# Moving the subtractions of a split-precision kernel from GpSimd to VectorE, and its gate the other way

## The chip, the core and the metric

The kernel runs on one core of one Trainium2 chip. Five engines work side by side, each with its own queue that it takes in order: TensorE (PE: matrix products and transposes), VectorE (DVE), ScalarE (ACT), GpSimd (POOL) and SyncE (SP), which issues nearly all DMAs. The metric is the time in microseconds that the device takes for one execution. Three executions took 1071.99, 1073.51 and 1075.36 us; their median is 1073.51 us.

## The reference

Three stages follow each other. Attention has 4 batches, 8 heads, 576 positions and 64 columns a head; a forget gate's running sum is a bias on the scores. Its output, 2304 tokens of 512 columns, runs through two layers with 2048 hidden columns each. The second layer's weights are as large as the first's.

```python
s_pos = np.maximum(s, 0.0)
cum = np.cumsum(s_pos, axis=-1)
bias = -(cum[:, :, :, None] - cum[:, :, None, :])
scores = np.where(causal, -1000000000.0, scores + np.minimum(bias, 0.0))
...
def _moe_ref(x, w_in, w_out, s, b):
    h = x @ w_in
    r = np.maximum(h, 0.0)
    g = s * (r * r) + b            # the gate: a scale and a bias, one number each
    return (g @ w_out).astype(np.float32)

def _moe2_ref(x, w_in, w_out, alpha):
    h = x @ w_in
    g = np.maximum(h, 0.0) + alpha * np.minimum(h, 0.0)
    return (g @ w_out).astype(np.float32)
```

The weights of the layers arrive as 64-bit floats, and the kernel reads them as pairs of 32-bit words.

## The kernel before

**Hi and lo parts.** TensorE multiplies in a reduced form of 32-bit floats. To keep the precision, a tensor x is split: ScalarE copies it into that form (hi), and another engine subtracts hi from x (lo). That is the helper `split` (L105 to L107): L106 is ScalarE's copy, L107 the subtraction, on VectorE unless the caller names GpSimd. A product of two split tensors is three products, hi by hi, hi by lo and lo by hi.

**Packets.** A packet is 128 of the hidden columns of a layer: a piece of w_in and a piece of w_out, 512 KB each, sixteen packets a layer. `load_packet` (L157) issues the two loads on SyncE (L174, L178), turns the 64-bit floats of each piece into 32-bit floats in `convert` (L116 on ScalarE, then L117 and L118 on VectorE), and splits them; here the lo parts are made on GpSimd (L191, and so L107 on POOL, tile w). Each piece is converted and split before the next.

**Blocks.** Tokens are taken 256 at a time (narrow) or 512 (wide). Layer 1 has seven narrow blocks and a last wide one, layer 2 one narrow block and four wide ones. `inputs` and `wide_inputs` (L547, L573) split a block's tokens. For each packet `up` (L623) multiplies the tokens by w_in into a PSUM tile hp (L634), and ScalarE takes it out with Relu (L653). In layer 1 ScalarE then squares it (L655) and VectorE applies the gate, times s plus b (L656), with s and b as columns of one number a partition; in layer 2 ScalarE takes the negative part out as well (L660) and VectorE joins the two (L661). The result r is split at L664 into gh and gl (tiles gh and gl in narrow blocks of layer 1, ring elsewhere; in the wide block of layer 1 the profile calls both ring). `down` (L667) multiplies gh and gl by w_out into accumulators (L673 in layer 1, L683 in layer 2), and it comes two packets after its `up` in layer 1, three in layer 2. Before the change the lo part gl is made on GpSimd in all of layer 1 and in layer 2's narrow block, and on VectorE in layer 2's wide blocks.

**Attention** works in units, a pair of heads by one of two ranges of rows. On VectorE it prepares the bias (L365), transposes q and k (L311), and joins scores and bias with a running minimum (L391); ScalarE takes the exponent (L397); on VectorE two small steps make the reciprocal of the sums (L402, L403), and GpSimd normalises (L406, tile probs), after which TensorE transposes (L437, tile pt) and multiplies by v (L453). GpSimd also masks (L369), clears (L361) and makes lo parts of v (tile vs_all).

**What sets the order.** The program is written as one stream in which attention and layer 1 alternate by a pace; the framework then reorders the instructions of each engine by a schedule of its own, which is made ahead of time and weighs each operation by the engine that it is on. So an operation that moves to another engine can shift everything around it, on all engines. Layer 1's first block and its sixteen packets stand beside attention's first batch; layer 2's packets are loaded and converted from the wide block of layer 1 on, into slots that layer 1's packets leave.

Of the kernel before, what the change touches and what calls it, by code (L numbers as in the profile page):

```python
# [8 lines left out]
F32 = mybir.dt.float32  # L9
# [9 lines left out]
def tile_forget_attention__then__two_mlps(  # L19
# [20 lines left out]
    nc = tc.nc  # L40
# [64 lines left out]
    def split(hi, lo, src, lo_eng=nc.vector):  # L105
        nc.scalar.copy(hi, src)  # L106
        lo_eng.tensor_tensor(out=lo, in0=src, in1=hi.bitcast(F32), op=ALU.subtract)  # L107
# [39 lines left out]
    def weight_tiles(f):  # L147

        if f not in SPARE:
            return [slot(n, F32R, f"w1_{f}_{n}") for n in SPLIT[SLOT[f]]]  # L150
        tiles = []
        for tag, pool, cols, n in SPARE[f]:
            t = pool.tile([P, cols], F32R, tag=tag, name=f"w1_{f}_{len(tiles)}")
            tiles += [t[:, i * 512 : (i + 1) * 512] for i in range(n)]
        return tiles

    def load_packet(layer, f):  # L157
        w_in, w_out = ((w_in1, w_out1), (w_in2, w_out2))[layer]


        def raw(name, n):
            if layer == 1:
                if f % 2:
                    tile_ = one.tile([P, 1024], U32, tag=("xh0", "xl0")[n], name=name)
                else:
                    tile_ = two.tile([P, 1088], U32, tag="probs", name=name)
            else:
                pool, tag = RAW[2 * f + n]
                tile_ = pool.tile([P, 1024], U32, tag=tag, name=name)
            return tile_[:, :1024].rearrange("p (n z) -> p n z", z=2)  # L170

        wi = raw(f"wi{layer}_{f}", 0)
        wo = raw(f"wo{layer}_{f}", 1)
        nc.sync.dma_start(  # L174
            out=wi.rearrange("p (c n) z -> p c (n z)", c=NCC),
            in_=w_in[:, f * 2 * P : (f + 1) * 2 * P].rearrange("(c p) n -> p c n", p=P),
        )
        nc.sync.dma_start(out=wo.rearrange("p n z -> p (n z)"), in_=w_out[f * P : (f + 1) * P, :])  # L178
        t = weight_tiles(f) if layer == 1 else []
        for n, src in enumerate((wi, wo)):  # L180
            if layer == 1:
                pool, tag, cols = WT[(2 * f + n) % len(WT)]
                wt = pool.tile([P, cols], U32, tag=tag, name=f"wt{f}_{n}")[:, :512]
            elif (f, n) == (NF - 1, 1):
                wt = two.tile([P, 512], U32, tag="ph", name="last")
            else:
                wt = slot(WHOLE[f][n], U32, f"wt0_{f}_{n}")
            convert(src, wt)
            if layer == 0:
                t += [slot(m, F32R, f"w0_{f}_{len(t)}_{m}") for m in SPLIT[f][2 * n : 2 * n + 2]]  # L190
            split(t[2 * n], t[2 * n + 1], wt.bitcast(F32), nc.gpsimd)  # L191
        return [x.rearrange("p (c n) -> p c n", c=NCC) for x in t[:2]] + t[2:]


# [352 lines left out]
    def inputs(layer, t):  # L547

        first, count = SIZES[layer][t]
        if count == 2:  # L550
            return wide_inputs(layer, t, first)
        if layer == 0:
            src = xf.pop(t)
            xh = one.tile([P, NCC, T], F32R, tag=f"xh{t % 2}", name=f"xh{layer}_{t}")
            xl = one.tile([P, NCC, T], F32R, tag=f"xl{t % 2}", name=f"xl{layer}_{t}")
            xh, xl = ([x[:, c] for c in range(NCC)] for x in (xh, xl))
        else:
            src = one.tile([P, NCC, T], F32, tag="res", name=f"x2_{t}")
            nc.sync.dma_start(out=src, in_=x2_d[t].rearrange("p (c n) -> p c n", n=T))

            xh, xl = (
                [
                    two.tile([P, T], F32R, tag=tag, name=f"x{tag}{layer}_{t}_{c}", bufs=3 if c < 3 else 2)
                    for c, tag in enumerate(tags)
                ]
                for tags in (("gh", "gh", "gh", "r"), ("gl", "gl", "gl", "r"))
            )
        for c in range(NCC):
            on_pool = layer == 0 and (t or c % 2)
            split(xh[c], xl[c], src[:, c], nc.gpsimd if on_pool else nc.vector)  # L570
        return xh, xl

# [37 lines left out]
    def mlp_block(layer, t, x):  # L610
# [6 lines left out]
        first, count = SIZES[layer][t]  # L617
# [5 lines left out]
        def up(f):  # L623
# [7 lines left out]
            n = 0  # L631
# [21 lines left out]
            nc.scalar.activation(r, hs, AF.Relu, scale=1.0 / W_SCALE)  # L653
            if layer == 0:
                nc.scalar.square(r, r)  # L655
                nc.vector.tensor_scalar(  # L656
                    out=r, in0=r, scalar1=gate_s[:, 0:1], scalar2=gate_b[:, 0:1], op0=ALU.mult, op1=ALU.add
                )
            else:
                nc.scalar.activation(u, hs, AF.Relu, scale=-1.0 / W_SCALE)  # L660
                nc.vector.scalar_tensor_tensor(  # L661
                    out=r, in0=u, scalar=nalpha[:, f : f + 1], in1=r, op0=ALU.mult, op1=ALU.add
                )
            split(gh, gl, r, nc.gpsimd if layer == 0 or count == 1 else nc.vector)  # L664
            return gh, gl

        def down(f, g):  # L667
# [132 lines left out]
```

## Time and profile before

| what | value |
|---|---|
| median of three runs | 1073.51 us |
| the profiled execution | 1074.54 us, its span 1072.8 us |
| TensorE busy | 1027.5 us (96%) |
| VectorE busy | 643.1 us (60%) |
| ScalarE busy | 609.2 us (57%) |
| GpSimd busy | 469.4 us (44%) |
| the chain that ended last | PE 66%, DVE 14%, DMA 6%, issue 5%, ACT 4%, POOL 3% |

The shares are means over stages. TensorE is busy for nearly all of the time, but matmuls overlap and their ends are modelled, so its idle time, and what ends it, is read stage by stage. A wait is put down to the engine whose semaphore came last. The names in a row are those of the program's tiles: `w<-wt,w` on GpSimd is the lo part of a weight, made from the converted weight wt and its hi part, which shares the name w.

### The profile page before, as it was taken

What the parts mean: (1) busy time and instruction counts of PE and PEld (TensorE: products, weight loads), DVE (VectorE), ACT (ScalarE), POOL (GpSimd) and SP (SyncE); (2) the same over time, 40 slices, a digit from 0 to 9 for tenths busy, and PEclk for the clock granted to TensorE, in tenths of its full rate; (3) what the DMA queues carried; (4) which work ended last, traced back from release to release, by engine and by line L of the source; (5) the groups of instructions that cost most, each with busy time, mean ns of one, the idle gap of its engine ahead of it and who ended that gap; (6) DMA issues with size and microseconds to landing.
All of it is one profiled execution on the core that took longest, in us unless ns stands there. A gap on an engine that the chain in (4) does not pass through costs nothing.

```text
span 1072.8 us, 18363 instructions
## 1 busy us (share of the span) xinstructions
PE 1027.5 (96%) x6277; PEld 908.8 (85%) x6277; DVE 643.1 (60%) x1456; ACT 609.2 (57%) x1463; POOL 469.4 (44%) x848
## 2 busy tenths in 40 slices
PE   6798999899998999999999979999999999999998
PEld 4577789899998999999999758888888888888886
DVE  7899878777788887788862774623223223223222
ACT  3686767777776777767765566633334334323332
POOL 6778877665766666767653666520000000000000
PEclk9899899999999999999999999999999999999999
DMA  6897433332223231323222664301002001000001
GB/s 144 234 245 223 138 68 84 79 81 64 59 68 83 63 91 46 82 61 81 70 66 68 196 200 146 118 1 40 1 1 79 1 1 60 1 1 31 9 1 40
DMA packets 173758, 83.67 MB, mean 78 GB/s; under 512 B 135584, under 2 KB 161184, under 8 KB 173664
## 3 DMA queue, kind: packets, MB, share of 16 engines
q1 hardware_dynamic: 171984, 81.94, 28.7%
q8 instruction: 49, 0.80, 0.3%
q10 hardware_dynamic: 1680, 0.57, 0.3%
q14 instruction: 45, 0.37, 0.1%
HBM read 72.96 MB, written 9.51 MB: 77 GB/s over the span
## 4 chain that ended last, share of the span: by engine, by line
PE 66%; DVE 14%; DMA 6%; issue 5%; ACT 4%; POOL 3%; SPq 2%; DVEq 0%; POOLq 0%; ACTq 0%
PE hp L634 28%; PE acc L683 18%; PE acc L673 10%; PE pt L437 3%; PE av L453 3%; DVE probs L365 2%; DVE wt L118 2%; DVE xs L334 2%; DVE probs L391 2%; DMA wi<-in_moe_w_in_dram 1%; DMA wo<-in_moe_w_out_dram 1%; SPq L266 1%; DVE wt L117 1%; PE sc L390 1%; PE sc L389 1%
## 5 line engine op out<-in xcount | busy, mean ns | idle before, releaser
L634 PE MATMUL hp<-xh,w 128*128 128x256 f32 (+1 forms) x1536 | 399.5, 332 | 3.3 <-ACT r L653 3.3
L634 PEld LDWEIGHTS hp<-xh,w 128*128 128x128 f32 x1536 | 270.1, 191 | 30.4 <-ACT r L653 4.1
L634 PE MATMUL hp<-xl,w 128*128 128x256 f32 (+1 forms) x768 | 254.5, 331 | 0.0
L653 ACT ACTIVATE r<-hp 128x256 f32<-128x256 f32 (+1 forms) x208 | 96.3, 463 | 207.3 <-PE hp L634 203.6
L683 PE MATMUL acc<-w,ring 128*128 128x512 f32 x864 | 208.9, 390 | 0.7 <-ACT res L695 0.7
L683 PEld LDWEIGHTS acc<-w,ring 128*128 128x128 f32 x864 | 161.4, 188 | 34.2 <-ACT res L695 0.9
L661 DVE SCALAR_TENSOR_TENSOR r<-u,nalpha,r 128x512 f32<-128x512 f32 (+1 forms) x80 | 57.7, 722 | 219.0 <-ACT u L660 218.6
L673 PE MATMUL acc<-gh,w 128*128 128x256 f32 x896 | 177.2, 288 | 4.5 <-ACT gh L106 4.3
L634 PEld LDWEIGHTS hp<-xl,w 128*128 128x128 f32 x768 | 146.5, 191 | 14.2 <-POOL probs L361 0.7
L673 PEld LDWEIGHTS acc<-gh,w 128*128 128x128 f32 x896 | 140.9, 190 | 10.0 <-ACT gh L106 6.2
L673 PE MATMUL acc<-gl,w 128*128 128x256 f32 x448 | 130.0, 290 | 2.6 <-POOL gl L107 2.6
L406 POOL TENSOR_SCALAR probs<-probs,sm 64x64 f32<-64x64 f32 (+4 forms) x160 | 94.8, 606 | 61.4 <-DVE sm L403 59.2
L397 ACT ACTIVATE probs<-probs,nm 64x64 f32<-64x64 f32 (+4 forms) x160 | 90.0, 562 | 46.9 <-DVE nm L391 45.6
L107 POOL TENSOR_TENSOR w<-wt,w 128x512 fp32r<-128x512 f32 x63 | 89.1, 1420 | 38.8 <-ACT w L106 38.5
L107 POOL TENSOR_TENSOR gl<-r,gh 128x256 fp32r<-128x256 f32 x112 | 86.5, 772 | 34.7 <-ACT gh L106 33.5
L656 DVE TENSOR_SCALAR r<-r,gate_s,gate_b 128x256 f32<-128x256 f32 (+1 forms) x128 | 70.4, 550 | 42.8 <-ACT r L655 40.9
L106 ACT CAST ring<-r 128x512 fp32r<-128x512 f32 (+1 forms) x96 | 56.1, 584 | 68.2 <-DVE r L661 61.9
L673 PEld LDWEIGHTS acc<-gl,w 128*128 128x128 f32 x448 | 85.2, 190 | 4.8 <-POOL gl L107 4.4
L437 PE MATMUL pt<-ident,probs 128*128 128x128 f32 x480 | 77.3, 282 | 11.1 <-POOL probs L406 10.5
L391 DVE CUSTOM_DVE_ANT_0 probs<-sc,probs 128x320 f32<-128x320 f32 (+3 forms) x160 | 67.8, 427 | 16.7 <-PE sc L390 14.0
L365 DVE TENSOR_SCALAR probs<-cum,cumT 64x64 f32<-64x64 f32 (+4 forms) x160 | 68.7, 479 | 7.6 <-DMA cum<-cum_d 4.9
L437 PEld LDWEIGHTS pt<-ident,probs 128*128 128x128 f32 x480 | 56.4, 145 | 17.7 <-POOL probs L406 14.3
(91 smaller groups left out, 1623.6 us busy)
## 6 DMA issues: line engine op xcount, KB each, us to landing
wi<-in_moe_w_in_dram SPq DMA_DIRECT2D x32, 512.0 KB, 4.6
wo<-in_moe_w_out_dram SPq DMA_DIRECT2D x32, 512.0 KB, 4.7
cum<-cum_d SPq DMA_DIRECT2D x32, 288.0 KB, 3.4
cum<-cum_d SPq DMA_DIRECT2D x30, 160.0 KB, 3.1
nat<-in_k_dram SPq DMA_DIRECT2D x64, 72.0 KB, 2.3
x_d<-res SPq DMA_DIRECT2D x18, 256.0 KB, 2.2
out_dram<-res SPq DMA_DIRECT2D x18, 256.0 KB, 2.3
vn<-in_v_dram SPq DMA_DIRECT2D x32, 128.0 KB, 2.6
```

Of the source, the lines that this page charges most:

```text
L107: lo_eng.tensor_tensor(out=lo, in0=src, in1=hi.bitcast(F32), op=ALU.subtract)
L365: nc.vector.tensor_scalar(out=pt[:rows, :i1], in0=u.cums[h][:rows, :i1], scalar1=cumT[:rows, r, head : head + 1], scalar2=0.0, op0=ALU.sub ...
L391: nc.vector.tensor_tensor_reduce(out=pt[:rows, j0:j1], in0=scr, in1=pt[:rows, j0:j1], scale=-SCALE, scalar=init, op0=ALU.add, op1=ALU.min, ...
L397: nc.scalar.activation(pt[:rows, :n], pt[:rows, :n], AF.Exp, bias=nm[:rows, m : m + 1], scale=-1.0, accum_out=sm[:rows, m : m + 1],)
L406: nc.gpsimd.tensor_scalar(out=probs[r][:rows, :n], in0=probs[r][:rows, :n], scalar1=sm[:rows, m : m + 1], scalar2=1.0, op0=ALU.mult, op1=A ...
L437: nc.tensor.transpose(tp[:, o : o + P], u.probs[h][r][:, k0 : k0 + P], ident)
L634: nc.tensor.matmul(hs, a[:, c], b[c], start=(n == 0), stop=(n == len(terms) * NCC - 1))
L653: nc.scalar.activation(r, hs, AF.Relu, scale=1.0 / W_SCALE)
L656: nc.vector.tensor_scalar(out=r, in0=r, scalar1=gate_s[:, 0:1], scalar2=gate_b[:, 0:1], op0=ALU.mult, op1=ALU.add)
L661: nc.vector.scalar_tensor_tensor(out=r, in0=u, scalar=nalpha[:, f : f + 1], in1=r, op0=ALU.mult, op1=ALU.add)
L673: nc.tensor.matmul(banks[d] if count == 2 else acc[:, d], a[:, d * P : (d + 1) * P], b, start=(f == 0 and (d % 2 == 0 or count == 2) and n ...
L683: nc.tensor.matmul(banks[m], a[:, m * P : (m + 1) * P], b, start=(f == 0 and b is woh and a is gh), stop=(f == NF - 1 and a is gl),)
```

## The change

Four edits. In `load_packet` both pieces of a packet are converted first and split after, and the lo parts are made on VectorE. In `inputs` the first block's lo parts are all made on VectorE (half of them were on GpSimd). The gate of layer 1 is computed on GpSimd. The lo parts of r are made on GpSimd only in the narrow blocks of layer 1 after the first, and on VectorE in layer 1's first block, in its wide block and in all of layer 2.

```diff
         t = weight_tiles(f) if layer == 1 else []
+        values_ = []
         for n, src in enumerate((wi, wo)):
...
             convert(src, wt)
+            values_.append(wt.bitcast(F32))
+        for n, wt in enumerate(values_):
             if layer == 0:
                 t += [slot(m, F32R, f"w0_{f}_{len(t)}_{m}") for m in SPLIT[f][2 * n : 2 * n + 2]]
-            split(t[2 * n], t[2 * n + 1], wt.bitcast(F32), nc.gpsimd)
+            split(t[2 * n], t[2 * n + 1], wt)
...
         for c in range(NCC):
-            on_pool = layer == 0 and (t or c % 2)
+            on_pool = layer == 0 and t
             split(xh[c], xl[c], src[:, c], nc.gpsimd if on_pool else nc.vector)
...
                 nc.scalar.square(r, r)
-                nc.vector.tensor_scalar(
+                nc.gpsimd.tensor_scalar(
                     out=r, in0=r, scalar1=gate_s[:, 0:1], scalar2=gate_b[:, 0:1], op0=ALU.mult, op1=ALU.add
                 )
...
-            split(gh, gl, r, nc.gpsimd if layer == 0 or count == 1 else nc.vector)
+            split(gh, gl, r, nc.gpsimd if layer == 0 and t and count == 1 else nc.vector)
```

The schedule that sets the order comes out otherwise on every engine; three places follow. In names, a trailing number tells buffers apart; the numbers before it are packet, step or unit. Lines of the changed kernel are three further on (L391 is L394, L656 is L659).

VectorE in the start, before: from the first score step of attention's second pair of heads (sc_3) to the last one of the same head (sc_4_320).

```order
L391 ISA probs_1_1_0_912,nm_1_1_0_910<-sc_3_0_0_1_1_922,probs_1_1_0_912 128x448
L391 ISA nm_1_1_0_910 128x1
L117 TENSOR_SCALAR wt_5_1_1122<-wt_5_1_1122 128x512
L118 SCALAR_TENSOR_TENSOR wt_5_1_1122<-wo_5_1111,wt_5_1_1122 128x512
L391 ISA probs_1_1_0_912,nm_1_1_0_910<-sc_4_0_0_1_1_934,probs_1_1_0_912 128x320
L391 ISA nm_1_1_0_910 128x1
L391 ISA probs_1_1_0_912,nm_1_1_0_910<-sc_4_320_0_1_1_937,probs_1_1_0_912,nm_1_1_0_910 128x256
L391 ISA nm_1_1_0_910 128x1
```

The same place now, from the same first score step (sc_3) on:

```order
L394 ISA probs_1_1_0_912,nm_1_1_0_910<-sc_3_0_0_1_1_922,probs_1_1_0_912 128x448
L394 ISA nm_1_1_0_910 128x1
L107 TENSOR_TENSOR gl_0_0_821<-r_0_822,gh_0_0_820 128x256
L118 SCALAR_TENSOR_TENSOR wt_5_1_1118<-wo_5_1111,wt_5_1_1118 128x512
L117 TENSOR_SCALAR wt_6_1_1159<-wt_6_1_1159 128x512
L118 SCALAR_TENSOR_TENSOR wt_6_0_1155<-wi_6_1151,wt_6_0_1155 128x512
L406 RECIPROCAL sm_0_1_1_849<-sm_0_1_1_849 128x2
L107 TENSOR_TENSOR w_5_0_19_1123<-wt_5_0_1114,w_5_0_20_1122 128x512
L117 TENSOR_SCALAR wt_7_0_1208<-wt_7_0_1208 128x512
L118 SCALAR_TENSOR_TENSOR wt_6_1_1159<-wo_6_1152,wt_6_1_1159 128x512
L107 TENSOR_TENSOR gl_0_1_1103<-r_1_1104,gh_0_1_1102 128x256
L107 TENSOR_TENSOR w_5_2_21_1127<-wt_5_1_1118,w_5_2_22_1126 128x512
```

Before, two steps of one packet (wt_5_1) stood between the first and the second score step. Now thirteen rows stand between them (the first ten are shown): conversions of packets 5, 6 and 7, lo parts of weights (w_5_0) and the first block's lo part of r (gl_0_0).

GpSimd in layer 1's wide block, before: lo parts of the weights of layer 2 (w) and of r (ring) take turns.

```order
L107 TENSOR_TENSOR w_6_19_9529<-wt_0_9532,w_6_20_9528 128x512
L107 TENSOR_TENSOR w_5_13_9449<-wt_1_9456,w_5_14_9448 128x512
L107 TENSOR_TENSOR ring_9163<-r_7_9506,ring_9163 128x512
L107 TENSOR_TENSOR w_6_21_9531<-wt_1_9538,w_6_22_9530 128x512
L107 TENSOR_TENSOR w_7_23_9580<-wt_0_9583,w_7_24_9579 128x512
L107 TENSOR_TENSOR ring_9164<-r_8_9557,ring_9164 128x512
L107 TENSOR_TENSOR w_7_25_9582<-wt_1_9589,w_7_26_9581 128x512
```

Now GpSimd has only gates there, and VectorE makes both kinds of lo parts; this is VectorE at steps 8 and 9 of the wide block (r_8 is step 8):

```order
L118 SCALAR_TENSOR_TENSOR wt_0_9652<-wi_8_9644,wt_0_9652 128x512
L117 TENSOR_SCALAR wt_1_9656<-wt_1_9656 128x512
L118 SCALAR_TENSOR_TENSOR wt_1_9656<-wo_8_9645,wt_1_9656 128x512
L107 TENSOR_TENSOR w_8_27_9649<-wt_0_9652,w_8_28_9648 128x512
L117 TENSOR_SCALAR wt_1_9707<-wt_1_9707 128x512
L118 SCALAR_TENSOR_TENSOR wt_1_9707<-wo_9_9696,wt_1_9707 128x512
L107 TENSOR_TENSOR ring_9164<-r_8_9557,ring_9164 128x512
L107 TENSOR_TENSOR w_7_25_9582<-wt_1_9587,w_7_26_9581 128x512
```

The lo part of step 8 stands behind the conversions of packet 8 and of a half of packet 9, and ahead of a lo part of packet 7.

GpSimd in the middle, before, at two steps (r_7, r_8) of a narrow block:

```order
L406 TENSOR_SCALAR probs_2_1_1_6149<-probs_2_1_1_6149,sm_2_1_1_6148 128x448
L406 TENSOR_SCALAR probs_2_1_1_6149<-probs_2_1_1_6149,sm_2_1_1_6148 128x576
L107 TENSOR_TENSOR gl_4_7_6387<-r_7_6388,gh_4_7_6386 128x256
L361 MEMSET probs_3_1_1_6441 128x64
L107 TENSOR_TENSOR gl_4_8_6420<-r_8_6421,gh_4_8_6419 128x256
```

The same place now:

```order
L659 TENSOR_SCALAR r_8_6421<-r_8_6421,gate_s,gate_b 128x256
L409 TENSOR_SCALAR probs_2_1_1_6149<-probs_2_1_1_6149,sm_2_1_1_6148 128x448
L409 TENSOR_SCALAR probs_2_1_1_6149<-probs_2_1_1_6149,sm_2_1_1_6148 128x576
L107 TENSOR_TENSOR gl_4_8_6420<-r_8_6421,gh_4_8_6419 128x256
L659 TENSOR_SCALAR r_9_6632<-r_9_6632,gate_s,gate_b 128x256
```

The gate of step 8 now stands on GpSimd ahead of a pair of normalisations, and its lo part behind them.

## Rows read from the trace of the kernel before

**Rows 1.** Busy time by stage: us, then PE, PEld, DVE, ACT, POOL busy (instructions), clock, DMA.
```profile
0.00:125.00 125.00, 102.38 (x514) 76.65 (x514) 110.64 (x260) 81.43 (x209) 94.67 (x176) 0.93 0.78 206
125.00:550.00 425.00, 413.39 (x3353) 405.60 (x3353) 338.01 (x926) 311.27 (x844) 288.01 (x599) 1.00 0.31 70
550.00:700.00 150.00, 143.37 (x767) 121.61 (x766) 88.52 (x121) 91.79 (x187) 82.24 (x69) 0.98 0.44 141
700.00:1073.00 373.00, 368.33 (x1649) 304.96 (x1647) 105.90 (x151) 124.71 (x227) 4.46 (x6) 1.00 0.05 19
```

**Rows 2.** TensorE's waits, 0 to 125 us: us in total, times, longest.
```profile
PE pt L437 <- POOL probs L406: 7.0, 7, 2.0
PE acc L673 <- ACT gh L106: 2.5, 2, 1.9
PE acc L673 <- POOL gl L107: 1.2, 1, 1.2
```

**Rows 3.** TensorE's waits, 125 to 550 us.
```profile
PE pt L437 <- POOL probs L406: 3.5, 5, 2.4
```

**Rows 4.** TensorE's waits, 550 to 700 us.
```profile
PE acc L673 <- POOL ring L107: 4.2, 3, 2.4
PE acc L673 <- ACT ring L106: 1.6, 2, 1.1
```

**Rows 5.** The timeline in the wide block: start us, us, engine, line, operation [idle before].
```profile
601.52 0.43 DVE L117 TENSOR_SCALAR wt<-wt 128x512 uint32<-128x512 uint32 x1 [3.85 <-ACT wt L116]
601.98 0.69 DVE L118 SCALAR_TENSOR_TENSOR wt<-wo,wt 128x512 uint32<-128x512 uint32 x1
606.82 2.93 POOL L107 TENSOR_TENSOR w<-wt,w 128x512 fp32r<-128x512 f32 x2
608.50 1.52 DVE L117 TENSOR_SCALAR wt<-wt 128x512 uint32<-128x512 uint32 x1
612.73 1.48 POOL L107 TENSOR_TENSOR ring<-r,ring 128x512 fp32r<-128x512 f32 x1
612.98 1.78 DVE L118 SCALAR_TENSOR_TENSOR wt<-wi,wt 128x512 uint32<-128x512 uint32 x1
```

**Rows 6.** VectorE's groups, 0 to 125 us: count | busy us, mean ns | idle before.
```profile
L117 DVE TENSOR_SCALAR wt<-wt 128x512 uint32<-128x512 uint32 x30 | 20.1, 672 | 4.3 <-ACT wt L116 4.3
L118 DVE SCALAR_TENSOR_TENSOR wt<-wi,wt 128x512 uint32<-128x512 uint32 x15 | 16.2, 1080 | 0.2
L656 DVE TENSOR_SCALAR r<-r,gate_s,gate_b 128x256 f32<-128x256 f32 x9 | 5.8, 642 | 0.0
```

**Rows 7.** VectorE's groups, 555 to 700 us.
```profile
L117 DVE TENSOR_SCALAR wt<-wt 128x512 uint32<-128x512 uint32 x31 | 20.6, 668 | 21.1 <-ACT wt L116 21.1
```

**Rows 8.** GpSimd's groups, whole span.
```profile
L107 POOL TENSOR_TENSOR w<-wt,w 128x512 fp32r<-128x512 f32 x63 | 89.1, 1420 | 38.8 <-ACT w L106 38.5
L107 POOL TENSOR_TENSOR gl<-r,gh 128x256 fp32r<-128x256 f32 x112 | 86.5, 772 | 34.7 <-ACT gh L106 33.5 <-POOL ring L107 0.7
L107 POOL TENSOR_TENSOR ring<-r,ring 128x512 fp32r<-128x512 f32 x16 | 22.7, 1426 | 13.7 <-ACT ring L106 11.0 <-issue 2.3 <-POOL w L107 0.5
L406 POOL TENSOR_SCALAR probs<-probs,sm 128x192 f32<-128x192 f32 x32 | 15.2, 475 | 0.0
L406 POOL TENSOR_SCALAR probs<-probs,sm 128x320 f32<-128x320 f32 x32 | 17.4, 544 | 0.0
L406 POOL TENSOR_SCALAR probs<-probs,sm 128x448 f32<-128x448 f32 x32 | 24.7, 772 | 33.8 <-DVE sm L403 33.6
```

**Rows 9.** VectorE's groups, whole span.
```profile
L107 DVE TENSOR_TENSOR ring<-r,ring 128x512 fp32r<-128x512 f32 x64 | 44.3, 693 | 41.3 <-ACT ring L106 41.2
L107 DVE TENSOR_TENSOR xl<-xf,xh 128x256 fp32r<-128x256 f32 x6 | 2.9, 489 | 0.0
L656 DVE TENSOR_SCALAR r<-r,gate_s,gate_b 128x256 f32<-128x256 f32 x112 | 58.8, 525 | 30.7 <-ACT r L655 28.8 <-POOL probs L406 1.5
L656 DVE TENSOR_SCALAR r<-r,gate_s,gate_b 128x512 f32<-128x512 f32 x16 | 11.7, 728 | 12.1 <-ACT r L655 12.1
```

## The prediction

> **What bounds the kernel now.** I read the busy time by stage first, then the waits of TensorE in each stage, then the costs of the operations that the change moves. The stages [rows 1] show TensorE idle for 125.00 − 102.38 = 22.6 us before 125 us, 425.00 − 413.39 = 11.6 us from 125 to 550 us, 150.00 − 143.37 = 6.6 us from 550 to 700 us, and hardly at all after that, where layer 2's wide blocks run and GpSimd has next to nothing to do. So the change can work in the first 700 us only, and what it can win there is at most some 40 us. The three stages have different limits.
>
> The start (to 125 us) is short of VectorE: 110.64 of 125 us busy there, with attention units, weight conversions and the first gates all in one in-order queue. TensorE's longest wait in it is for GpSimd, which has 7.0 us for seven late normalisations, and its waits for the first gated tiles' hi and lo parts add 2.5 and 1.2 us [rows 2]. The DMA engines are busy but not full: 0.78 of the start, at a mean of 206 GB/s [rows 1].
>
> The middle (to 550 us) is TensorE at 97%. What it waits for is spread thin: 3.5 us for GpSimd's normalisations is the longest [rows 3]. The third stage (550 to 700 us) holds the wide block of layer 1 and the narrow block of layer 2, with all sixteen packets of layer 2 being converted beside them. TensorE waits there 4.2 us for lo parts that GpSimd makes and 1.6 us for hi parts [rows 4].
>
> **What GpSimd's subtractions do to VectorE.** This is the row that decides most. At 601 to 602 us a packet's two VectorE steps take 0.43 and 0.69 us. A few us later, started while GpSimd subtracts, the same step of L117 takes 1.52 us and that of L118 1.78 us; they end 0.3 and 0.6 us after GpSimd's subtraction has ended, as if they had mostly stood waiting for it [rows 5]. The means over the start are 672 ns for L117 and 1080 ns for L118 (its fifteen on the first half of a packet; the fourteen on the second are taken alike) [rows 6], and 668 ns for L117 over the third stage [rows 7]. The excess over the undisturbed steps is, in the start, 30 x (672 − 430) = 7.3 and 29 x (1080 − 690) = 11.3 us: 19 us of 110.6. In the third stage it is 31 x 238 = 7.4 us for L117, and some 11 us for 32 of L118 if they stand as in the start.
>
> **The lo parts of the weights.** They take 64 subtractions of 1420 ns off GpSimd, half in the start and half in the third stage, and give VectorE as many of 693 ns, the row of the same shape with no GpSimd work beside it [rows 8, 9]. For VectorE that is 29 x 0.693 = 20.1 us more up to 125 us, against the 19 us of excess that goes with the subtractions: no change within 2 us. For GpSimd it is 29 x 1.42 = 41 us less of 94.67. The new places in line count as well: the order shows a score step of attention with thirteen VectorE rows ahead of it where two stood, and packets taken earlier.
>
> **The gate, and the lo parts of the intermediates.** The gate leaves VectorE 128 times. In the start it is 9 x 642 ns = 5.8 us [rows 6], and the sixteen lo parts of the first block come in its place at 489 ns [rows 9], 7.8 us. No row shows the gate's form, with two column operands, on GpSimd. Its neighbours there are the normalisation of 192 columns at 475 ns and of 320 at 544 ns, so halfway, 510 ns for 256; 448 columns take 772 ns [rows 8], so about 820 for 512. From above, the subtraction of 256 columns bounds it at 772 ns; from below, 475. I take 510 and 820. The gate's step in the chain of a narrow block then costs as much as on VectorE, and there its consumer is two steps of the layer behind, so it is hidden by TensorE's own work.
>
> **Start: −7 us.** VectorE's sum is 20.1 − 19 − 5.8 + 7.8, 3 us more than before. With that and GpSimd relieved by 41 us and by the first block's subtractions (14 x 0.77 us, less 14 x 0.51 us for gates), the waits that go are those for GpSimd: 7.0 + 1.2 us, of which a late sum ahead of a normalisation may keep some. In the order's first place the first block's lo parts of steps 0 and 1 come before the second score step, so TensorE has that block's products to do while a score is late. Bounds: 0, if VectorE stays as late as now, and −22, all of the idle time. I take −7, next to the row.
>
> **Middle: −1 us.** About 92 gates move. At 525 ns [rows 9] VectorE is rid of 48 us of its 338, and GpSimd gets 92 x 0.51 = 47 us onto 288, which makes 335 of 425 (79%) [rows 1]. Behind a gate on GpSimd wait the normalisations and the lo part; the normalisations are what TensorE waited 3.5 us for [rows 3]. Bounds: −3.5, if that wait goes, and +12, if one gate in four delays a step by 0.5 us. I take −1, since two steps of slack (8.7 us at 92 steps in 400 us) are longer than a gate, a pair of normalisations and a lo part in line on GpSimd (0.51 + 2 x 0.77 + 0.77 = 2.8 us).
>
> **Third stage: −4.5 us.** Each of the 16 wide lo parts becomes 1426 − 693 = 733 ns shorter and stands no more behind subtractions of weights [rows 8, 9]; the gate goes to an otherwise empty GpSimd. VectorE adds 32 x 0.693 + 16 x 0.693 + 10 x 0.489 = 38 us and loses 16 gates of 728 ns (11.6 us), the 18 us of excess above and what else waits for GpSimd's subtractions; of its 150 us it has 88.52 busy, so it comes to some 97. Of the waits of 4.2 and 1.6 us [rows 4] I let 4.5 go. What is late next is VectorE's line itself: a lo part behind a conversion whose load has not landed. Bounds: −6.6, all of the idle time, and +6, if each of twelve lo parts comes 0.5 us late.
>
> **The sum.** 1074.5 us (the profiled execution) − 7 − 1 − 4.5 = 1062.0 us. The median of the runs stands 1.0 us below that execution, so I predict 1061 us.
>
> **A rule that speaks against it.** In the Trainium skill, "SBUF — State Buffer", section "Who interferes with whom", a VectorE instruction with two SBUF inputs, or in a mode with two ports, and a GpSimd instruction that reads SBUF exclude each other, the later one waiting in full. The long steps beside GpSimd's subtractions agree [rows 5]. By it the new subtractions on VectorE and the gates on GpSimd exclude each other too. The holding time, from rows, falls from 64 x 1.42 + 16 x 1.43 + 32 x 0.77 to 112 x 0.51 + 16 x 0.82 us, 138 to 70 us; it moves into the middle, where VectorE has over 100 us free, and so I leave the sum as it is.
>
> **Rivals.** *Slower: VectorE's line in the start.* The excess of L117 and L118 does not come from the subtractions but from GpSimd's other work, and stays. Then VectorE has 20.1 + 7.8 − 5.8 = 22 us more to do in a stretch that has 14 us free, and attention's scores stand behind weights: some 15 us later at its end, less the 4.5 us: 1074.5 + 15 − 4.5 − 1 = 1084, 1083 as a median. For it speaks that VectorE is full there; against it rows 5, where the long steps end just behind GpSimd's. It decides if L118 still averages over 0.9 us. *No change: the loads.* The packets come no earlier than the queue brings them, scores wait behind conversions that wait for a load, and the third stage gains no more than 2 us: 1072. For it speaks that the DMA engines are busy for 0.78 of the start, more than twice the middle's share; against it that none of TensorE's long waits there ends with a load. *More than forecast.* With the start's TensorE fed by an earlier first block, 15 of 22.6 us go, all 5.8 us of the third stage and 3 of the middle: 1074.5 − 24 = 1051, 1050 as a median. For it speaks that both side engines shed work: GpSimd 138 − 70 = 68 us, VectorE 70 us of gates against 64 x 0.693 + 16 x 0.693 + 32 x 0.489 = 71 us of lo parts and the excess on top. *The gate on GpSimd costs more than its neighbours.* At 772 ns for 256 columns GpSimd stands at 359 of 425 us in the middle, and some of the +12 us comes in: 1070.
>
> **How the numbers follow.** Forecast 0.53, more than forecast 0.20, no change by the loads 0.11, the dear gate 0.06, slower 0.10. The forecast's own range is 1056 to 1068. To hold 8 in 10 it must take in the larger gain and part of the no-change case: 1049 to 1074. A measurement of this kernel tells a difference of about 0.3% (3.2 us) from none, so faster is below 1070.3 us: forecast, the larger gain and half of the dear gate, 0.76. Within: 0.13. Slower: 0.11.
>
> **What would show it.** Right: L117 near 430 ns and L118 near 700 ns in both stages; TensorE's wait for normalisations in the start well under 7 us, and its idle time before 125 us under 17 us; no wait for a lo part over 1 us between 600 and 650 us; the gate on GpSimd at 480 to 560 ns. Wrong: L118 over 0.9 us; VectorE over 115 of the first 125 us with TensorE waiting for scores; waits for hi parts in the middle over 5 us.

## The result: 1064.7 us, and where it came from

The changed kernel takes 1064.73 us (median of four runs, 1063.57 to 1066.16) against 1072.94 us for the kernel before in the same comparison: a ratio of 0.9914 [0.9895, 0.9934], 8.2 us faster. I had predicted 1061 us. The profiled execution took 1066.16 us, its span 1064.4 us, 8.4 us less than before.

The profile after, busy time by stage, with the columns of [rows 1]:

```profile
0.00:125.00 125.00, 107.56 (x572) 84.33 (x573) 101.01 (x283) 84.55 (x216) 60.25 (x144) 0.92 0.74 203
125.00:550.00 425.00, 409.62 (x3271) 398.52 (x3270) 299.47 (x840) 307.81 (x830) 326.87 (x682) 0.99 0.31 71
550.00:700.00 150.00, 150.00 (x843) 130.69 (x842) 91.08 (x168) 98.76 (x201) 29.61 (x37) 1.00 0.44 141
```

Subtract TensorE's busy time from each stage, as for [rows 1]. Its idle time is 17.4, 15.4 and 0.0 us where it was 22.6, 11.6 and 6.6: −5.2, +3.8 and −6.6, together −8.0 us. That is the change of the span within half a microsecond, and from 700 us on both executions idle for 4.5 us, so nothing is hidden in the last stage. By 550 us the idle time adds up to 32.8 us, and before it was 34.2: nearly all of what the change wins is won in the third stage. The start's win is mostly given back in the middle.

TensorE's waits after, 0 to 125 us (total, times, longest), to set beside [rows 2]:

```profile
PE pt L440 <- POOL probs L409: 5.8, 3, 3.4
PE tp L102 <- POOL probs L364: 4.8, 1, 4.8
```

And 125 to 550 us, beside [rows 3]:

```profile
PE pt L440 <- POOL probs L409: 6.6, 5, 2.8
PE hp L637 <- ACT r L656: 2.6, 4, 1.0
PE av L456 <- DVE pl L107: 2.5, 5, 0.8
PE acc L676 <- POOL gl L107: 1.6, 3, 0.9
```

In the start the waits of [rows 2] for gh and gl are gone and the one for normalisations is 1.2 us shorter. The wait of 4.8 us in the second row is not new: it is the one before TensorE's first work, and before, it was put down to another engine:

```profile
PE tp L102 <- DVE cum L97: 4.7, 1, 4.7
```

In the middle the wait for normalisations has grown from 3.5 to 6.6 us, and the one for lo parts of the transposed scores on VectorE (pl) from 1.0 to 2.5 us. From 550 to 700 us the view has no wait left in place of [rows 4].

VectorE's groups after, 0 to 125 us, beside [rows 6]:

```profile
L107 DVE TENSOR_TENSOR w<-wt,w 128x512 fp32r<-128x512 f32 x31 | 22.1, 713 | 1.0 <-ACT w L106 0.7
L117 DVE TENSOR_SCALAR wt<-wt 128x512 uint32<-128x512 uint32 x31 | 14.7, 476 | 4.4 <-ACT wt L116 4.3
L118 DVE SCALAR_TENSOR_TENSOR wt<-wi,wt 128x512 uint32<-128x512 uint32 x16 | 12.2, 761 | 0.0
```

And 550 to 700 us, beside [rows 7]:

```profile
L107 DVE TENSOR_TENSOR w<-wt,w 128x512 fp32r<-128x512 f32 x32 | 23.0, 722 | 6.1 <-ACT w L106 5.9
L117 DVE TENSOR_SCALAR wt<-wt 128x512 uint32<-128x512 uint32 x32 | 14.2, 445 | 19.1 <-ACT wt L116 18.7
L118 DVE SCALAR_TENSOR_TENSOR wt<-wi,wt 128x512 uint32<-128x512 uint32 x16 | 11.0, 690 | 0.3
```

L118 before, 550 to 700 us, which [rows 7] leave out:

```profile
L118 DVE SCALAR_TENSOR_TENSOR wt<-wi,wt 128x512 uint32<-128x512 uint32 x16 | 17.5, 1092 | 0.4
```

The step of L117 fell from 672 to 476 ns in the start and from 668 to 445 ns in the third stage, that of L118 from 1080 to 761 ns and from 1092 to 690 ns. In the third stage VectorE took 32 subtractions of weights and 16 of the wide block and is busy for 91.1 us, 2.6 us more than before. The new work is paid for by the gates that left (15.5 us there) and by steps that no longer stand waiting.

They are not the conversions alone. Two of attention's steps on VectorE in the start, before (the bias, L365, and the first step on the sums, L402):

```profile
L365 DVE TENSOR_SCALAR probs<-cum,cumT 128x576 f32<-128x576 f32 x7 | 6.6, 944 | 0.0
L402 DVE TENSOR_SCALAR sm<-sm 128x3 f32<-128x3 f32 x8 | 4.2, 528 | 0.7 <-ACT probs L397 0.6
```

After:

```profile
L368 DVE TENSOR_SCALAR probs<-cum,cumT 128x576 f32<-128x576 f32 x6 | 3.1, 516 | 0.0
L405 DVE TENSOR_SCALAR sm<-sm 128x3 f32<-128x3 f32 x8 | 1.4, 170 | 0.0
```

GpSimd's gates after, whole span:

```profile
L659 POOL TENSOR_SCALAR r<-r,gate_s,gate_b 128x256 f32<-128x256 f32 x112 | 78.1, 698 | 46.9 <-ACT r L658 40.8 <-DVE nm L394 3.3 <-DMA wo<-in_moe_w_out_dram 1.2
L659 POOL TENSOR_SCALAR r<-r,gate_s,gate_b 128x512 f32<-128x512 f32 x16 | 15.3, 958 | 63.3 <-ACT r L658 51.9 <-DVE wt L118 9.5 <-DVE ring L107 1.9
```

The gate costs 698 ns in the mean where I took 510, and 958 where I took 820. Half of the 128 gates take 557 ns or less.

**Where the start's win went.** ScalarE's exponents (L397 before, L400 after) count how far attention has come. Before, by stretch: us, busy us and count, then the clock and the DMA columns.

```profile
0.00:150.00 150.00, 28.92 (x89) 0.94 0.71 184
150.00:300.00 150.00, 27.88 (x86) 0.99 0.32 71
300.00:550.00 250.00, 47.81 (x145) 1.00 0.30 69
```

After:

```profile
0.00:150.00 150.00, 27.05 (x83) 0.93 0.66 178
150.00:300.00 150.00, 27.73 (x86) 0.97 0.32 73
300.00:550.00 250.00, 49.39 (x150) 1.00 0.31 72
```

TensorE does 572 matmuls in the start where it did 514, but attention is six exponents behind at 150 us and makes them up after 300 us. By 550 us TensorE has 3843 matmuls recorded against 3867 before. More of layer 1 was done early, and more of attention was left for later.

### The profile page after: what moved, and what is told of

Read it like the earlier page. It is cut to its first block, busy times and chain, and to the rows that moved or that the text cites. A ratio compares the mean times of both kernels' runs of the same rounds, so it can differ in the third digit from the quotient of the medians.

```text
span 1064.4 us, 18248 instructions
## 1 busy us (share of the span) xinstructions
PE 1027.1 (97%) x6277; PEld 910.8 (86%) x6277; DVE 597.2 (56%) x1442; ACT 612.5 (58%) x1463; POOL 416.7 (39%) x862
## 4 chain that ended last, share of the span: by engine, by line
PE 78%; DVE 6%; DMA 5%; ACT 3%; POOL 3%; issue 2%; SPq 2%; DVEq 0%; POOLq 0%; ACTq 0%
PE hp L637 33%; PE acc L686 18%; PE acc L676 15%; PE av L456 4%; PE pt L440 4%; PE sc L390 1%; DVE probs L368 1%; PE sc L393 1%; DMA wo<-in_moe_w_out_dram 1%; SPq L269 1%; PE sc L392 1%; POOL r L659 1%; DVE probs L394 1%; DMA nat<-in_k_dram 1%; DVE turned L314 1%
## 5 line engine op out<-in xcount | busy, mean ns | idle before, releaser
L656 ACT ACTIVATE r<-hp 128x256 f32<-128x256 f32 (+1 forms) x208 | 96.2, 463 | 205.4 <-PE hp L637 203.4
L637 PEld LDWEIGHTS hp<-xl,w 128*128 128x128 f32 x768 | 145.9, 190 | 13.2 <-issue 0.7
L659 POOL TENSOR_SCALAR r<-r,gate_s,gate_b 128x256 f32<-128x256 f32 (+1 forms) x128 | 93.4, 730 | 110.2 <-ACT r L658 92.7
L400 ACT ACTIVATE probs<-probs,nm 64x64 f32<-64x64 f32 (+4 forms) x160 | 89.9, 562 | 39.0 <-DVE nm L394 38.2
L409 POOL TENSOR_SCALAR probs<-probs,sm 64x64 f32<-64x64 f32 (+4 forms) x160 | 91.3, 582 | 35.6 <-DVE sm L406 28.2
L107 DVE TENSOR_TENSOR ring<-r,ring 128x512 fp32r<-128x512 f32 (+1 forms) x96 | 62.1, 647 | 61.6 <-ACT ring L106 61.3
L394 DVE CUSTOM_DVE_ANT_0 probs<-sc,probs 128x320 f32<-128x320 f32 (+3 forms) x160 | 67.9, 427 | 45.8 <-PE sc L393 32.9
L107 POOL TENSOR_TENSOR gl<-r,gh 128x256 fp32r<-128x256 f32 x96 | 74.6, 777 | 16.2 <-ACT gh L106 15.9
L440 PEld LDWEIGHTS pt<-ident,probs 128*128 128x128 f32 x480 | 57.4, 147 | 20.8 <-POOL probs L409 14.9
```

Source lines behind the costliest of these rows:

```text
L394: nc.vector.tensor_tensor_reduce(out=pt[:rows, j0:j1], in0=scr, in1=pt[:rows, j0:j1], scale=-SCALE, scalar=init, op0=ALU.add, op1=ALU.min, ...
L400: nc.scalar.activation(pt[:rows, :n], pt[:rows, :n], AF.Exp, bias=nm[:rows, m : m + 1], scale=-1.0, accum_out=sm[:rows, m : m + 1],)
L409: nc.gpsimd.tensor_scalar(out=probs[r][:rows, :n], in0=probs[r][:rows, :n], scalar1=sm[:rows, m : m + 1], scalar2=1.0, op0=ALU.mult, op1=A ...
L440: nc.tensor.transpose(tp[:, o : o + P], u.probs[h][r][:, k0 : k0 + P], ident)
L637: nc.tensor.matmul(hs, a[:, c], b[c], start=(n == 0), stop=(n == len(terms) * NCC - 1))
L659: nc.gpsimd.tensor_scalar(out=r, in0=r, scalar1=gate_s[:, 0:1], scalar2=gate_b[:, 0:1], op0=ALU.mult, op1=ALU.add)
```

## The experiments

All ran beside the kernel before on the same chip. The theory held that GpSimd's subtractions hold VectorE up, and that taking them away wins time in the start and in the third stage. Its rivals were that the gate or the smaller lo parts bring the gain, and that the order of the work does. Every edit makes the order anew, so no run holds it fixed. TensorE's idle time is worked out by stage as above; beside it stands its busy time. Each ratio is to the runs of before that were taken beside that kernel; their medians lie between 1072.27 and 1073.38 us. Idle and busy time come from one execution each. The busy time differs by up to 7.8 us between kernels that do the same products, so a difference of 2 or 3 us in the median is not read from one stage alone.

| kernel | median us | ratio to before [95%] | idle 0–125 | 125–550 | 550–700 | busy, whole span |
|---|---|---|---|---|---|---|
| before | 1072.94 | | 22.6 | 11.6 | 6.6 | 1027.5 |
| the change | 1064.73 | 0.9914 [0.9895, 0.9934] | 17.4 | 15.4 | 0.0 | 1027.1 |
| weights_only | 1066.30 | 0.9931 [0.9912, 0.9950] | 17.0 | 15.2 | 1.1 | 1027.1 |
| gate_only | 1082.81 | 1.0084 [1.0062, 1.0105] | 24.1 | 13.2 | 10.7 | 1028.3 |
| parts_only | 1077.18 | 1.0028 [1.0008, 1.0048] | 23.4 | 14.2 | 3.6 | 1027.7 |
| no_gate | 1071.71 | 0.9985 [0.9967, 1.0003] | 24.0 | 13.6 | 0.4 | 1023.6 |
| no_weights | 1079.44 | 1.0061 [1.0037, 1.0085] | 23.0 | 15.5 | 6.2 | 1028.8 |
| first_weights | 1073.35 | 1.0006 [0.9989, 1.0023] | 18.7 | 16.0 | 5.2 | 1025.7 |
| late_only | 1060.69 | 0.9894 [0.9875, 0.9913] | 22.3 | 10.2 | 0.0 | 1021.0 |
| hold | 1079.83 | 1.0069 [1.0044, 1.0094] | 24.1 | 14.7 | 4.9 | 1026.3 |
| late_weights | 1062.03 | 0.9892 [0.9864, 0.9921] | 20.8 | 9.5 | 1.0 | 1023.5 |
| late_no_gate | 1060.54 | 0.9882 [0.9856, 0.9908] | 20.1 | 9.4 | 0.0 | 1026.3 |
| change_again | 1064.42 | 0.9919 [0.9893, 0.9945] | 18.2 | 16.4 | 0.0 | 1024.2 |

### Each part alone

**weights_only**: of the kernel before, only the lo parts of the weights move. Both pieces of a packet are converted first here too, as in every kernel below that touches the weights.

```diff
             convert(src, wt)
+            values_.append(wt.bitcast(F32))
+        for n, wt in enumerate(values_):
...
-            split(t[2 * n], t[2 * n + 1], wt.bitcast(F32), nc.gpsimd)
+            split(t[2 * n], t[2 * n + 1], wt)
```

> Only the lo parts of the weights move to VectorE (both pieces of a packet converted first, as in the change); the gate stays on VectorE and the other lo parts where they were. Theory (GpSimd's subtractions of weights hold VectorE's steps up): L117 falls to 420 to 480 ns and L118 to 690 to 760 ns, the start and the third stage give back most of what the change gave (5.2 and 6.6 us), the middle is as before: 1062 to 1067 us. Rival (the gain came from taking the gate off VectorE, and the order that follows): VectorE has 20 us more in a start that was full, so 1074 us or slower.

It took 1066.30 us, −7.1 us against the 1073.38 us of before there: nearly the whole gain, with the idle times of the change in every stage within 1.1 us. Three signs missed. The middle is not as before (15.2 us idle for 11.6). L117 averages 492 ns in the start, just over its range. And L118 stays over its 760 ns, at 846 ns on wi in the start and 788 in the third stage (VectorE's groups, 550 to 700 us):

```profile
L107 DVE TENSOR_TENSOR w<-wt,w 128x512 fp32r<-128x512 f32 x32 | 28.7, 901 | 8.3 <-ACT w L106 8.0
L118 DVE SCALAR_TENSOR_TENSOR wt<-wi,wt 128x512 uint32<-128x512 uint32 x16 | 12.6, 788 | 0.4
```

Here the lo parts of r are still made on GpSimd, and VectorE's own subtractions take 901 ns for the 722 of the change. So part of the holding is left.

**gate_only**: only the gate moves.

```diff
-                nc.vector.tensor_scalar(
+                nc.gpsimd.tensor_scalar(
```

> Only the gate of layer 1 moves to GpSimd. Theory: the excess of L117 and L118 stays (672 and 1080 ns in the start), and the middle loses what it lost in the change, some 4 us, for GpSimd's line: 1072 to 1079 us. Rival (the gate off VectorE is what paid): 1064 to 1069 us with the start's idle time of TensorE at 18 us or less.

It is 9 us slower, more than forecast, and the middle lost 1.6 us of idle time and not some 4. L118 stayed long, as forecast (1036 ns on wi in the start, 1104 in the third stage). TensorE's waits in its third stage:

```profile
PE acc L673 <- ACT ring L106: 5.6, 3, 3.8
PE acc L683 <- ACT res L695: 3.6, 1, 3.6
PE acc L673 <- POOL ring L107: 1.5, 2, 0.8
```

ScalarE's hi part comes behind the gate, and here the gate stands on GpSimd in one line with subtractions of weights of 1.4 us each. A wait put down to ScalarE came up from 1.6 us [rows 4] to 5.6 us. That the line is the reason is read from the order, not shown by itself. In the change, where the subtractions are gone, no such wait is left.

**parts_only**: only the lo parts of the tokens and of r move.

```diff
-            on_pool = layer == 0 and (t or c % 2)
+            on_pool = layer == 0 and t
...
-            split(gh, gl, r, nc.gpsimd if layer == 0 or count == 1 else nc.vector)
+            split(gh, gl, r, nc.gpsimd if layer == 0 and t and count == 1 else nc.vector)
```

> Only the lo parts of the intermediates and of the first block's tokens move to VectorE. Theory: TensorE's waits of 4.2 us for the lo parts in the wide block shrink, since a lo part no longer stands behind subtractions of weights, but those still hold VectorE, where the lo part now is; so between 0 and 3 us: 1070 to 1074 us. Rival (the third stage's gain came from these lo parts and not from the weights): 1066 to 1068 us and no idle time of TensorE from 550 to 700 us.

It is 3.8 us slower, a miss. The third stage gains 3.0 us of idle time, but the middle loses 2.6 and the start 0.8. The three parts alone make −7.1, +9.4 and +3.8 us; together they make −8.2. They don't add.

### The change without one part

**no_weights**: the change with the weights' lo parts on GpSimd.

```diff
-            split(t[2 * n], t[2 * n + 1], wt)
+            split(t[2 * n], t[2 * n + 1], wt, nc.gpsimd)
```

> The change with the lo parts of the weights left on GpSimd: gate on GpSimd, lo parts of intermediates and first block's tokens on VectorE. Theory: without the weights nothing is won, and the gates of the wide block stand behind subtractions on GpSimd: third stage idle 5 to 10 us, 1074 to 1083 us. Rival (gate and lo parts changing places is what paid): 1064 to 1069 us.

Without the weights nothing is left of the gain: 1079.44 us, and 6.2 us of idle time in the third stage, both as forecast. The reason given, gates that stand behind subtractions, is not what the waits show there: TensorE waits 5.0 us in all for lo parts of r on VectorE, which take 1003 ns each beside GpSimd's subtractions and 689 in the change.

**no_gate**: the change with the gate on VectorE.

```diff
-                nc.gpsimd.tensor_scalar(
+                nc.vector.tensor_scalar(
```

> The change without its gate: the lo parts of weights, intermediates and first block's tokens on VectorE, the gate on VectorE as before. Theory (the gate on GpSimd costs the middle some 4 us and helps neither of the other stages much): 1059 to 1064 us, the middle's idle time of TensorE back at 11 to 13 us. Rival (VectorE needs the gate taken off to carry the lo parts): its start is over 112 us busy of 125, and 1068 us or slower.

It took 1071.71 us, a miss. Its profiled execution took 1067.80 us, 3.9 us less than the median, so the stages tell less here. Against the change TensorE idles 6.6 us more in the start, 1.8 less in the middle and 0.4 more in the third stage. Its waits in the start:

```profile
PE pt L440 <- POOL probs L409: 11.2, 5, 4.7
PE tp L102 <- POOL probs L364: 4.8, 1, 4.8
```

VectorE is busy for 99.6 of those 125 us and GpSimd for 50.0, so neither is full; attention has 79 exponents by 150 us, the fewest of all with those of hold. The order differs from the change's on every engine, and which row of it makes those normalisations late I have not found.

### Start and third stage apart

**first_weights**: only layer 1's weights, those of the start.

```diff
+            split(t[2 * n], t[2 * n + 1], wt, nc.vector if layer == 0 else nc.gpsimd)
```

> Only the lo parts of layer 1's weights move to VectorE; those of layer 2 stay on GpSimd, and so do the gate (VectorE) and the other lo parts as before. Theory (the whole gain is in the third stage; what the start wins, attention gives back before the last narrow block of layer 1 is over): the last step of that block starts at 570 to 574 us, the third stage keeps 5 to 8 us of idle TensorE: 1072 to 1078 us. Rival (the start's 5 us are kept to the end): 1066 to 1070 us.

This is the run that decides on the start. Busy time by stage, first two stages, columns as in [rows 1]:

```profile
0.00:125.00 125.00, 106.27 (x579) 83.43 (x580) 108.16 (x286) 83.81 (x218) 61.32 (x147) 0.93 0.75 204
125.00:550.00 425.00, 409.05 (x3280) 399.68 (x3279) 326.54 (x925) 307.14 (x829) 278.21 (x591) 0.99 0.32 71
```

TensorE idles 3.9 us less in the start and 4.4 us more in the middle, and the time is the same: 1.0006 [0.9989, 1.0023]. No gate was moved here, so the middle's loss is not the gate's. Attention has 83 exponents by 150 us, as in the change, and TensorE's longest wait in the middle is for normalisations, as there:

```profile
PE pt L440 <- POOL probs L409: 6.6, 7, 2.2
```

In the third stage, where layer 2's subtractions are on GpSimd, L117 averages 759 ns and L118 962 ns on wi, though both pieces are converted first. So it is not the converting first that shortens them. The forecast's other mark, the last step of the last narrow block at 570 to 574 us (568 to 571 in late_only), was not met: the block's last gate starts at 578.0 us here, at 580.4 in late_only and at 583.3 before. Steps of the wide block stand between, so the mark says little.

**late_only**: only what lies in the third stage: layer 2's weights, the lo parts of the wide block and of layer 2, and the wide block's gates.

```diff
+            split(t[2 * n], t[2 * n + 1], wt, nc.gpsimd if layer == 0 else nc.vector)
...
+                (nc.gpsimd if count == 2 else nc.vector).tensor_scalar(
...
+            split(gh, gl, r, nc.gpsimd if layer == 0 and count == 1 else nc.vector)
```

> The change from the wide block of layer 1 on alone: layer 2's weights and the lo parts of the wide block and of layer 2 on VectorE, the wide block's gate on GpSimd; layer 1's weights, first block and narrow gates as before. Theory: the last narrow block's last step starts at 568 to 571 us as before, TensorE idles under 1 us from 550 to 700 us: 1061 to 1065 us, at least as fast as the whole change. Rival (the start's part is worth 5 us of its own): 1067 to 1070 us.

It is 11.6 us faster than before, 0.3 us below the range expected. The third stage has no idle time left, the middle 10.2 us where the change has 15.4, and the start is as before. Its idle time over the span, 37.3 us, is that of the change; what it has over the change in this execution is busy time, 1021.0 against 1027.1 us, at a mean granted clock of 0.992 against 0.985. The next three runs tell more.

**late_weights**: of those, only layer 2's weights (the first of the three lines). **late_no_gate**: the first and the third. **change_again**: the change once more beside them.

> Only the lo parts of layer 2's weights move to VectorE; all else as before the change. Theory (these 32 subtractions are the cause by themselves): TensorE idles under 2 us from 550 to 700 us, and the time is within 3 us of the kernel with all late edits: 1060 to 1064 us. Rival (the wide block's lo parts on VectorE and its gate on GpSimd carry half of it): 1065 to 1069 us.

> All late edits but the gate: layer 2's weights, the wide block's lo parts and those of layer 2 on VectorE, the gate on VectorE everywhere. Theory (the third stage already has next to no idle TensorE, so the gate has nothing left to win there): within 2 us of the kernel with the wide block's gate on GpSimd, 1059 to 1063 us. Rival (the gate off VectorE is what lets it carry the lo parts): 1065 us or slower, and TensorE idles over 2 us from 550 to 700 us.

> The change as it is, beside the kernels with late edits alone on one chip. Theory (the start's part of the change wins nothing that lasts): 1063 to 1067 us, 2 to 6 us over the late edits alone. Rival (the late edits alone were lucky in their order): 1059 to 1062 us, no more than 1 us over them.

The three forecasts held. Moving layer 2's 32 subtractions alone brings −11.1 us, and the lo parts of r 1.5 us more by the medians, which lies within their spread. Late_no_gate, from 125 to 700 us, columns as in [rows 1]:

```profile
125.00:550.00 425.00, 415.56 (x3366) 407.08 (x3365) 337.31 (x932) 314.56 (x850) 292.15 (x603) 1.00 0.32 71
550.00:700.00 150.00, 150.00 (x835) 130.33 (x834) 97.06 (x184) 95.85 (x197) 6.77 (x9) 1.00 0.44 140
```

The wide gates on GpSimd win nothing: with them 1060.69, without 1060.54 us. Against change_again the six runs of late_no_gate are 3.9 us faster in the mean (from their spread, 95%: 1.1 to 6.8 us). Here the idle time shows it: 34.0 us over the span, 11.3 less than before and 5.0 less than in change_again. So late_no_gate is faster than both the one before and the change. But of these 11.3 us only 6.6 are in the third stage, where layer 2's subtractions run (5.6 in late_weights). The other 4.7 are in the start and the middle, where only the order and the converting first differ. No run tells these two apart.

### The holding by itself

**hold**: no_gate, plus one subtraction on GpSimd for each of layer 2's 32 pieces, hi minus hi, into a tile that nothing reads. What the kernel computes is unchanged.

```diff
+    spent = const.tile([P, 512], mybir.dt.bfloat16, name="spent")
...
+            if layer == 1:
+                nc.gpsimd.tensor_tensor(out=spent, in0=t[2 * n].bitcast(F32), in1=t[2 * n].bitcast(F32), op=ALU.subtract)
```

> The change without its gate, and for each piece of layer 2's weights one more subtraction on GpSimd, of a hi part from itself into a tile that nothing reads: 32 of them, of the length of those that were taken off, and no result waits for them. Theory (the subtractions hold VectorE's steps up by being there): in the third stage L117 goes from 445 ns up to 550 to 700 ns and L118 from 690 ns to 850 to 1100 ns, TensorE idles 2 to 6 us there, and the time is 2 to 6 us over the kernel without them, 1074 to 1078 us. Rival (what was slow was only the wait for the lo parts that GpSimd made): both steps stay within 30 ns of 445 and 690 ns, and the time within 2 us of 1071.7 us.

VectorE's groups of no_gate, 555 to 700 us:

```profile
L107 DVE TENSOR_TENSOR w<-wt,w 128x512 fp32r<-128x512 f32 x32 | 22.0, 689 | 1.9 <-ACT w L106 1.8
L117 DVE TENSOR_SCALAR wt<-wt 128x512 uint32<-128x512 uint32 x32 | 13.6, 425 | 9.8 <-ACT wt L116 9.4
L118 DVE SCALAR_TENSOR_TENSOR wt<-wi,wt 128x512 uint32<-128x512 uint32 x16 | 11.5, 720 | 0.3
```

The same of hold, where the lines are one further on:

```profile
L108 DVE TENSOR_TENSOR w<-wt,w 128x512 fp32r<-128x512 f32 x32 | 31.2, 976 | 1.5 <-ACT w L107 1.4
L118 DVE TENSOR_SCALAR wt<-wt 128x512 uint32<-128x512 uint32 x32 | 18.0, 571 | 7.3 <-ACT wt L117 7.0
L119 DVE SCALAR_TENSOR_TENSOR wt<-wi,wt 128x512 uint32<-128x512 uint32 x16 | 12.9, 808 | 0.3
```

And what was added, on GpSimd:

```profile
L197 POOL TENSOR_TENSOR spent<-w 128x512 bf16<-128x512 f32 x32 | 43.3, 1354 | 69.2 <-ACT w L107 66.7 <-PE hp L640 1.3
```

Nobody waits for these subtractions, and yet VectorE's own subtractions grow from 689 to 976 ns and the two steps from 425 to 571 and from 720 to 808 ns; VectorE is busy for 122.1 instead of 102.8 us from 550 to 700 us. TensorE's idle time there goes from 0.4 to 4.9 us, with a wait that no_gate does not have:

```profile
PE acc L679 <- DVE ring L108: 2.6, 3, 1.8
```

The time goes from 1071.71 to 1079.83 us. Of the 8.4 us between the two profiled executions, 4.4 are this idle time; 1.1 are idle time in the middle, 2.7 are busy time, and no row ties these to the extra subtractions. Before 125 us the two kernels idle alike, 24.0 and 24.1 us. The forecast missed in two sizes: the step on wi stayed under its 850 ns, and the time went above its 1078 us. VectorE's subtractions took most of the waiting, which fits with their place beside the extra ones, but that is argued. That GpSimd's subtractions, by their presence alone, lengthen VectorE's work is shown. The Trainium skill ("SBUF — State Buffer", section "Who interferes with whom") names a VectorE instruction with two SBUF inputs and a GpSimd instruction that reads SBUF as contending, and the rows agree: 689 to 976 ns.

## Why the prediction was right, and which of its steps were not

**The holding: right.** The excess on L117 and L118 went with the subtractions: in the start 31 x (476 − 430) + 16 x (761 − 690) + 15 x (702 − 690) = 2.7 us are left of the 19 (702 ns is the mean on wo). The rival that it comes from GpSimd's other work, to be told by L118 over 0.9 us, is out: 761 and 690 ns. Some of it seems to come from GpSimd's other subtractions: with only the weights moved, L118 still averaged 846 and 788 ns. The rival of the loads, to be told by a third stage that gains no more than 2 us, is out as well: it gained 6.6, with the DMA engines as busy as before (0.44).

**Third stage, −4.5 us: right in kind, too small.** It measured −6.6 us, all of the idle time. I had left 2.1 us for VectorE's line, a lo part behind a conversion; with VectorE busy for 91.1 of 150 us, no wait for it is left in the view.

**Start, −7 us: the step that failed.** TensorE's idle time fell by 5.2 us there, close to the number, but the sum took it as time won. first_weights shows that it isn't: 3.9 us in the start, back as 4.4 us in the middle, no gain. What TensorE had in place of idling was layer 1's work. Each of the six kernels with layer 1's weights on VectorE has 79 to 84 exponents by 150 us, each of the other seven 89. VectorE in the start came out 9.6 us less busy, where I had 3 us more. The sum counted the excess on the conversions alone, but attention's bias and sums had it too: over all their shapes they took 26.8 us before and 16.5 after, for nearly as many instructions (52 and 49). Beside that, some of attention's work moved behind 125 us, five score steps among it.

**Middle, −1 us: wrong in sign, +3.8 us.** I counted only the gate there. GpSimd grew by 38.9 us and VectorE lost 38.5, where the sum had 47 and 48, and slack did hide most of it: gate_only, with the gate's cost but no weights, has only 1.6 us more idle time there. The loss comes with the start's weights, without any gate (first_weights +4.4, weights_only +3.6). That it comes *through* attention's delay is argued from the counts and the waits: in the middle TensorE waits 4.9 to 6.7 us for normalisations in the six kernels with layer 1's weights on VectorE, and 1.9 to 3.7 in the other seven. There is another way to the same loss: no_weights idles 15.5 us with 89 exponents at 150 us and 2.3 us of that wait, but waits 4.6 us for pl and 2.9 us for a lo part of r on VectorE.

**The gate at 510 ns: too low, harmless.** It is 698 ns in the mean. The rival of the dear gate, at 772 ns, gave 1070 us; the gate alone costs more than that (gate_only), but in its company it saved time (no_gate 1071.7 against 1064.7 us). I had no step that could say so. Its place seems to be the start, where the order differs; what in that order does it stays open.

**The sum.** The terms were off by 1.8 us in the start, 4.8 in the middle and −2.1 in the third stage, 4.5 us in all; the profiled execution, 1066.2 against 1062.0 us, is off by 4.2. The middle is the term that made the forecast too low. The start and the middle together were to bring 8 us and brought 1.4, and the third stage brought 2.1 more than its term, so that the number came out within 4 us is in part luck; the wide range took in much else.

**The signs.** Met: L118 near 700 ns, L117 near 430 in the third stage, no wait for a lo part between 600 and 650 us. Not met: the gate at 480 to 560 ns in the mean, and TensorE's idle time under 17 us in the start, by 0.4 us. Two stand between: L117 in the start at 476 ns, and the wait for normalisations there at 5.8 us. None of the signs of being wrong came up.

## What to carry to other kernels

Count what an engine's instructions cost the engine beside it: 32 subtractions moved off GpSimd left TensorE 5.6 us less idle time in the stage where they run (late_weights), though VectorE took all of them on. Idle time that goes in an early stage is won only if the later stages don't give it back, so add up the idle time to the end, and count the progress of the work that could have been pushed aside. Where a schedule is made anew with each edit, try the parts singly and by stage: here the part of the change that concerns the third stage, without its gate, is better than the whole (late_no_gate).

## What the runs showed that I had not expected

The holding seems to work both ways. Two gates of the wide block in the changed kernel, in the timeline (start us, us, engine, operation):

```profile
612.03 1.95 DVE L107 TENSOR_TENSOR w<-wt,w 128x512 fp32r<-128x512 f32 x3
612.83 1.62 POOL L659 TENSOR_SCALAR r<-r,gate_s,gate_b 128x512 f32<-128x512 f32 x1 [2.81 <-ACT r L658]
613.90 0.83 DVE L117 TENSOR_SCALAR wt<-wt 128x512 uint32<-128x512 uint32 x1
619.15 0.77 POOL L659 TENSOR_SCALAR r<-r,gate_s,gate_b 128x512 f32<-128x512 f32 x1 [4.69 <-DVE wt L118]
```

The gate that runs from 612.83 us, beside three subtractions of VectorE, takes 1.62 us, and ends 0.5 us after the third. VectorE's step behind them, L117, starts while that gate runs, takes 0.83 us for its usual 0.43 and ends 0.3 us after the gate. The one that starts at 619.15 us, with the end of a step of VectorE, takes 0.77. So I read the 698 and 958 ns of the gates as a price of 0.55 us (the shortest on 256 columns took 0.54) and of 0.77 us with waiting on top; no run was made to show it. The change moved the subtractions away from GpSimd and put the gate into the same kind of place.
